# An mLSTM cell that updates its carried state every 64 tokens in place of every 128, in front of a squared-ReLU FFN

## The chip, the cores and the metric

The kernel runs on one core of one Trainium2 chip. The metric is the device time of one execution in microseconds (us); lower is better. Three timed runs of the kernel before are shown, and one further execution was taken with the hardware profiler; all durations below come from that one.

The core has five engines with a queue of their own each, and each queue is worked off in the order in which it was written: TensorE (PE, matmuls; its weight loads are shown as PEld), VectorE (DVE), ScalarE (ACT), GpSimd (POOL) and SyncE (SP, which here issues transfers). An instruction that waits holds up everything behind it in its own queue.

## The reference

There are 4 batches of 8 heads, 768 tokens and 40 dimensions per head. For every head a 40x40 state C and a normaliser n are carried over the tokens, with a running maximum m for stability, and the result goes through a two-layer FFN:

```python
for t in range(S):
    m_new = np.maximum(f_gate[:, :, t] + m, i_gate[:, :, t])
    f_stab = np.exp(f_gate[:, :, t] + m - m_new)
    i_stab = np.exp(i_gate[:, :, t] - m_new)
    m = m_new
    C = f_stab * C + i_stab * np.einsum('bhd,bhe->bhde', vt, kt)
    n = f_stab * n + i_stab * kt
    h_tilde = np.einsum('bhde,bhe->bhd', C, qt)
    nq = np.einsum('bhd,bhd->bh', n, qt)
    y[:, :, t] = sigmoid(o) * h_tilde / np.maximum(np.abs(nq), 1.0)
x = y as (4*768 tokens, 8*40)
out = np.maximum(x @ w_in, 0) ** 2 @ w_out          # w_in 320x2048, w_out 2048x320
```

Everything is float32. A recurrence of this kind can be worked off in blocks of tokens: inside a block, the output is (scores of q and k) x (a matrix W of decays, zero above the diagonal) x v; what came before the block enters as q, scaled by the decay since the block's start, times the carried C; and C is brought to the block's end once per block. n rides along as a 41st column of v that holds ones.

## The kernel before, in words

The 3072 tokens are worked off in 24 chunks of 128 (`s` is the chunk, `c = s % 6` its place in its batch), each with all 8 heads. In chunk `s` the steps are:

- `load_A`, `mask`, `decays`, `weigh`: the running log decays `A` are spread over the partitions, masked above the diagonal (POOL), exponentiated (ACT) into `eA` (the decay since the chunk's start, for q) and into W. From chunk 8 (`ROT`) on, W is laid out in 64-row halves: 192 columns a head pair, made of the two 64x64 blocks on the diagonal and the full block below it; the fourth block is zero and left out.
- `scores`: 16 matmuls of a 64x64 quarter of the array each, four of which run side by side; `weighted` (DVE) multiplies scores by W and gives P.
- `scale_q` (DVE) multiplies `eA` by q, `decay_C` (POOL) multiplies the old state by the decay over the chunk, which gives `Cd`, and `values` (POOL) scales v by the last column of W, which gives `vw`.
- `attend_begin` and `attend_end` (PE) make the output in two PSUM banks `numT`: `values_of_C` (scaled q times the old C), `values_of_P` (P times v) and `new_C` (k times `vw`). Each of the three is split over the two calls, because the two halves of a sum would otherwise be added to the same place of a bank at once. A DVE instruction on one element (the `tensor_scalar` into `spare`, line 790) stands between the two calls: it reads the last result of the first half, and the second half waits for it.
- At the end of `attend_end`, two DVE transposes (line 853) turn the output for `store_num`, and two DVE additions (line 860) write the new state, `dC + Cd`.

The order of all engines' work is written out by hand: a loop over `parts`, four steps (`at` 0 to 3) per chunk from chunk 6 on. Even chunks run beside the second FFN layer (`ffn2_fast`, line 1056), odd ones beside the first (`ffn1_open` and `ffn1_close`, line 1132, and `ffn1_rows`, line 1165), which uses Strassen-like sums made on DVE and POOL. `attend_begin` and `attend_end` stand at step 1. Between the two calls PE has other work: in an even chunk the scores of the next chunk, in an odd chunk `ffn1_rows`:

```python
if at == 1:
    do(attend_begin, s)
    if even:
        do(lambda s: scores(s, ("h", "h")), s + 1)
    if fast:
        ffn1_rows(g, 0, True)
    do(attend_end, s)
    do(decays, s + 1)
    do(mask, s + 1)
    ...
    do(decay_C, s + 1)
```

What else the change and the prediction touch:

- POOL also issues transfers: in step 3 of every even chunk `pair_up` twice (8 issues, line 343) and `load` (7 issues, lines 363 to 375), and in chunk 9, straight behind them, `spread_slots` (3 issues, lines 383 and 385; also once before chunk 6 and once in chunk 12). All of these stand in POOL's queue ahead of what the next odd chunk gives to POOL. `sums_of_x` (lines 1124 and 1127) stands just before them.
- `ffn1_open` fills four of the five PSUM banks of the pool `ps_h` (X, Y, V, Z); `ffn1_close` adds to X, Y and V, and then one ACT and four DVE instructions (lines 1182 to 1185) read them out. The next `ffn1_open` takes the fifth bank for its X and then X's, Y's and V's old banks in turn; its two DVE additions are lines 1148 and 1150.
- `keep` is a constant of ones and zeros; the scan that sums log decays restarts where it is zero, at every 128th token.

## Time and profile before

| what | value |
|---|---|
| timed runs, median (lowest to highest) | 486.21 us (484.28 to 487.42) |
| the profiled execution's own time | 486.42 us |
| its span, first to last instruction | 484.7 us |
| around the span | 1.7 us |
| granted TensorE clock | 1.00 |
| PE, DVE, ACT, POOL busy, share of the span | 98%, 71%, 50%, 46% |
| chunks 8 to 23, place in the span | about 124 to 409 us |

Busy shares are averages over the whole span. A float32 matmul shows as two records, so 16 matmuls are 32 entries in a group or a timeline. In a timeline, a row gives the start, the time from the first start to the last end, engine, line, operation, operands and the number of records; the brackets hold the idle time of the engine before it and what ended it. Because neighbouring matmuls overlap, the price of a run of them is read from its start to the start of the next run.

### The profile page before, as it was taken

To read this page: it belongs to the slowest core of one execution; us is meant where nothing else is said; L and a number is where in the kernel's file an instruction comes from. 1 tells how busy PE (TensorE), PEld (TensorE's weight loads), DVE (VectorE), ACT (ScalarE), POOL (GpSimd) and SP (SyncE) were. 2 spreads that over 40 slices of the span, in tenths; PEclk is the share of its full clock that TensorE was granted. 3 is DMA by queue.
4 is the path that set the end of the run, shared out by engine and by line. 5 is a ranking of instruction groups with operands and counts; after the bars stand their busy time and mean duration, and the time that the engine had idled before them with its cause. 6 is when DMAs were issued, how large, how long until landed. Compare 5 with 4: busy or idle time off the path is not lost.

```text
span 484.7 us, 15567 instructions
## 1 busy us (share of the span) xinstructions
PE 476.5 (98%) x6307; PEld 443.9 (92%) x6309; DVE 342.4 (71%) x722; ACT 243.2 (50%) x534; POOL 224.9 (46%) x336
## 2 busy tenths in 40 slices
PE   8999999999999999999999999999999999999997
PEld 4886787779999999999999999999999999999997
DVE  7979868798897866767775956857966956635441
ACT  4699799634743723923622931742942741513300
POOL 5464544656598096098097088089083040020000
PEclk9999999999999999999999999999999999999999
DMA  8999998788977776777677758849655612200000
GB/s 174 200 261 248 284 210 207 213 151 201 183 148 197 141 149 177 135 151 178 129 132 197 139 98 223 142 98 225 126 110 143 126 46 84 57 28 3 1 27 28
DMA packets 192696, 69.93 MB, mean 144 GB/s; under 512 B 158128, under 2 KB 181360, under 8 KB 192624
## 3 DMA queue, kind: packets, MB, share of 16 engines
q1 hardware_dynamic: 186400, 58.68, 56.0%
q0 software_dynamic: 6080, 10.16, 8.6%
q8 instruction: 50, 0.82, 0.7%
q14 instruction: 22, 0.18, 0.1%
q10 hardware_dynamic: 144, 0.10, 0.1%
HBM read 55.69 MB, written 18.92 MB: 154 GB/s over the span
## 4 chain that ended last, share of the span: by engine, by line
PE 83%; DMA 5%; DVE 4%; ACT 3%; SPq 2%; issue 1%; POOL 1%; DVEq 0%; POOLq 0%; ACTq 0%
PE h_ps L1056 32%; PE h_ps L1132 24%; PE h_ps L1165 7%; PE h_ps L972 4%; PE h_ps L1010 4%; PE numT L819 3%; PE numT L799 2%; ACT g_c L515 1%; PE numT L830 1%; DMA num_rows<-tn 1%; DMA kqT<-kq_rows 1%; PE h_ps L983 1%; PE tp L594 1%; PE h_ps L586 1%; PE tp L586 1%
## 5 line engine op out<-in xcount | busy, mean ns | idle before, releaser
L478 POOL TENSOR_SCALAR_AFFINE_SELECT A_bc<-A_bc 64x512 f32<-64x512 f32 x32 | 23.1, 721 | 88.1 <-ACT kq L496 59.3
L1146 ACT COPY r_sb<-h_ps 128x512 f32<-128x512 f32 x20 | 11.7, 585 | 84.6 <-PE h_ps L1132 84.6
L1056 PE MATMUL h_ps<-T,S 128*128 128x160 f32 x352 | 51.7, 300 | 0.0
L1056 PEld LDWEIGHTS h_ps<-T,S 128*128 128x128 f32 x352 | 48.9, 190 | 0.4 <-ACT g L1181 0.2
L1056 PE MATMUL h_ps<-w_out,g 128*128 128x160 f32 x336 | 49.2, 303 | 0.0
L1056 PEld LDWEIGHTS h_ps<-w_out,g 128*128 128x128 f32 x336 | 46.1, 190 | 1.3 <-issue 0.9
L1072 DVE TENSOR_TENSOR y_sb<-y_sb,h_ps 128x160 f32<-128x160 f32 x44 | 14.0, 318 | 45.2 <-PE h_ps L1056 45.0
L1132 PE MATMUL h_ps<-xT,w_in 128*128 128x128 f32 x320 | 43.4, 278 | 0.7 <-issue 0.7
L1132 PE MATMUL h_ps<-lent_t,w_in 128*128 128x128 f32 x320 | 42.3, 275 | 0.0
L1132 PEld LDWEIGHTS h_ps<-xT,w_in 128*128 128x128 f32 x320 | 39.2, 192 | 1.6 <-issue 1.2
L1132 PEld LDWEIGHTS h_ps<-lent_t,w_in 128*128 128x128 f32 x320 | 38.9, 192 | 0.8 <-issue 0.8
L375 POOL DMA_DIRECT2D va<-in_v_dram x64 | 39.3, 626 | 0.0
L1165 PE MATMUL h_ps<-xT,w_in 64*64 64x128 f32 x960 | 39.2, 272 | 0.0
L1132 PE MATMUL h_ps<-lent_t 128*128 128x128 f32 x320 | 39.1, 275 | 0.0
L1132 PEld LDWEIGHTS h_ps<-lent_t 128*128 128x128 f32 x320 | 37.3, 192 | 0.2 <-issue 0.2
L509 ACT ACTIVATE A_bc<-A_bc,b_R 128x64 f32<-128x64 f32 (+1 forms) x128 | 35.7, 361 | 1.0 <-POOL A_bc L478 0.6
L1165 PEld LDWEIGHTS h_ps<-xT,w_in 64*64 64x64 f32 x960 | 34.8, 133 | 1.3
L853 DVE STREAM_TRANSPOSE tn<-numT 128x256 f32<-128x256 f32 x36 | 14.0, 428 | 27.9 <-PE numT L799 18.9
L1124 POOL TENSOR_TENSOR lent_t<-xT 128x128 f32<-128x128 f32 (+1 forms) x18 | 15.6, 887 | 32.7 <-DVE xT L938 32.7
L972 PE MATMUL h_ps<-xT,w_in 128*128 128x256 f32 x128 | 30.1, 386 | 0.5 <-POOL w_in L236 0.4
L1056 PE MATMUL h_ps<-w_out,g_c 128*128 128x160 f32 x192 | 28.0, 302 | 0.0
L972 PEld LDWEIGHTS h_ps<-xT,w_in 128*128 128x128 f32 x128 | 23.4, 190 | 5.0 <-POOL w_in L236 1.3
(233 smaller groups left out, 1148.1 us busy)
## 6 DMA issues: line engine op xcount, KB each, us to landing
A_bc<-a_slots SPq DMA_DIRECT2D x32, 256.0 KB, 4.3
kq<-num_rows SPq DMA_DIRECT2D x80, 64.0 KB, 2.2
num_rows<-tn SPq DMA_DIRECT2D x18, 256.0 KB, 2.5
raw<-in_moe_w_out_dram SPq DMA_DIRECT2D x7, 640.0 KB, 5.7
kqT<-kq_rows SPq DMA_DIRECT2D x34, 128.0 KB, 3.8
og<-in_o_gate_dram SPq DMA_DIRECT2D x24, 160.0 KB, 4.9
x_rows<-x_sb SPq DMA_DIRECT2D x20, 192.0 KB, 3.4
xT<-x_rows SPq DMA_DIRECT2D x80, 48.0 KB, 3.3
```

What stands on the lines that cost most here:

```text
L375: eng.dma_start(dst[HALVES[n], PR * (1 - late_keys) : PR * (2 - late_keys)], src[HALVES[late_keys], PR * m : PR * (m + 1)],)
L478: nc.gpsimd.affine_select(part, part, compare_op=ALU.is_ge, fill=-1e30, base=0, pattern=[[0, PR], [0, 2], [1, DP]], channel_multiplier=-1,)
L509: nc.scalar.activation(A[0][:, x, to], A[0][:, x, to], AF.Exp, bias=b_R[:, b, c, own, x : x + 1],)
L819: nc.tensor.matmul(d["numT"][m][HALVES[e], i, t0:], lhsT=va_w[s % NKQ][keys, at * D1 : at * D1 + DP], rhs=rhs, start=(s % NB == 0 and i == ...
L853: nc.vector.transpose(to[:, 2 * m : 2 * m + 2], d["numT"][m].rearrange("p c t -> p (c t)"))
L972: nc.tensor.matmul(hs[i][:, n, :], lhsT=w_in[:, a, fb * P : (fb + 1) * P], rhs=xT[:, :, a, :], start=(n == 0 and a == 0), stop=False,)
L1010: nc.tensor.matmul(st["o_ps"][j], lhsT=st["g2", 0][:, fb, j * P : (j + 1) * P], rhs=w_out[:, fb, :], start=(fb == 0), stop=(fb == NF - 1),)
L1056: nc.tensor.matmul(to, lhsT=lhsT[:, p], rhs=rhs[:, p, :], start=(start and p == 0), stop=(p == NPAIR - 1), skip_group_check=True,)
L1072: add = lambda to, a, b: nc.vector.tensor_tensor(to, a, b, op=ALU.add)
L1124: sub = lambda to, a, b: eng.tensor_tensor(to, a, b, op=ALU.subtract)
L1132: nc.tensor.matmul(to[:, n, :], lhsT=lhsT[:, 4 * q + n, :], rhs=rhs, start=(start and n == 0), stop=True, skip_group_check=True,)
L1165: nc.tensor.matmul(to[cols, n, :], lhsT=w_in2[rows, 4 * q + n, cols], rhs=rhs, start=(start and n == 0), stop=True, skip_group_check=True,)
```

## The change

From chunk 8 on, the state is brought up to date after each 64 tokens. The log decays now restart at every 64th token (`keep`). Of the scores, of W and of P only the two 64x64 blocks on the diagonal are made, 128 columns a head pair in place of 192; the block below the diagonal is replaced by a second product with the state. So `attend_begin` and `attend_end` give way to `sub_begin` and `sub_end` for these chunks. `sub_begin` issues the first half's product with C, three of the four groups of P times v, and both halves of k times `vw`; then DVE adds the first half's `dC` to `Cd` and writes the state at token 64 to `mid` (which takes the place of `eA_T`, not used any more by then), and POOL multiplies `mid` by the second half's decay, which `keep_last` put aside, into a new `Cd`. `sub_end` issues the second half's products with `mid`, the rest of the first half's with C, the last of P, four transposes in place of two, and the two additions that make the new state. The one-element instruction of line 790 is gone from these chunks. The first chunk of a batch (`c == 0`) now also needs `decays`, `scale_q` and products with `mid`, and the last (`c == 5`) also `values` and the first half's k times `vw`.

```diff
--- before.py
+++ after.py
@@ -130,6 +130,12 @@
             nc.gpsimd.memset(t[:, H * D1 :], 0.0)
         nc.vector.memset(keep[:], 1.0)
         nc.vector.memset(keep[:, :, 0:1], 0.0)
+        for x in range(NX):
+            rows, whole = slice((x + 1) * BH, (x + 2) * BH), H * -(-(ROT - 2 * x) // NB)
+            nc.gpsimd.affine_select(
+                keep[rows, :, DP : DP + 1], keep[rows, :, DP : DP + 1], compare_op=ALU.is_ge, fill=0.0, base=whole - 1,
+                pattern=[[0, SX // P], [0, 1]], channel_multiplier=-1,
+            )
         make_identity(nc, ident[:])
 
         nc.gpsimd.memset(sel[:], 0.0)
@@ -482,7 +488,7 @@
 
     def decays(s):
 
-        if s % NB > 0:
+        if s % NB > 0 or s >= ROT:
             home = kq_b[2 + s % 2 if s >= NB else s - X_SQ - 1]
             e = st[s]["eA"] = home[:, 1].rearrange("p (j two) d -> p j (two d)", two=2)
             for i in range(2):
@@ -505,7 +511,7 @@
         if len(A) == 1 and not masked:
             mask(s)
         for x in range(PR if s >= ROT else 0):
-            for own, to in enumerate((slice(DP, P), slice(P, 2 * P))):
+            for own, to in enumerate((slice(DP, P), slice(P, P + DP))):
                 nc.scalar.activation(
                     A[0][:, x, to], A[0][:, x, to], AF.Exp, bias=b_R[:, b, c, own, x : x + 1],
                 )
@@ -523,10 +529,10 @@
     def values(s):
         b, c = divmod(s, NB)
         d = st[s]
-        if c + 1 < NB:
+        if c + 1 < NB or s >= ROT:
             d["vw"] = prep.tile([P, H, D1], F32, name="vw")
             if s >= ROT:
-                last = d["W"][:, :, P - 1 :: P].rearrange("p x own -> p own x")
+                last = d["W"][:, :, P - 1 : P + DP : DP].rearrange("p x own -> p own x")
                 nc.gpsimd.tensor_tensor(
                     d["vw"][:].rearrange("p (own x) d -> p own x d", own=2),
                     d["va"][:].rearrange("p (own x) d -> p own x d", own=2),
@@ -569,7 +575,7 @@
         d["sc"] = sc
         if s >= KQ_SQ:
             if s >= ROT:
-                d["sc"] = [t.rearrange("p j t -> p (j t)")[:, : 3 * P].rearrange("p (e t) -> p e t", e=2) for t in sc]
+                d["sc"] = [t.rearrange("p j t -> p (j t)")[:, : 2 * P].rearrange("p (e t) -> p e t", e=2) for t in sc]
             for e in range(2):
                 for late_keys in range(2):
                     for c in range(2):
@@ -577,14 +583,14 @@
                             rows = slice(DP * i, DP * i + D)
                             start = e == late_keys == 0
                             if s < ROT:
-                                j, keys = 2 * late_keys + e, HALVES[c]
-                                to, t0 = sc[i][HALVES[c], j, :], 0
+                                j, keys, toks = 2 * late_keys + e, HALVES[c], slice(0, P)
+                                to = sc[i][HALVES[c], j, :]
                             else:
                                 j, keys = 2 * (c ^ late_keys) + e, HALVES[late_keys]
-                                to = d["sc"][i][HALVES[c], e, slice(0, DP) if late_keys else slice(DP, 3 * DP)]
-                                t0 = DP * late_keys
+                                to = d["sc"][i][HALVES[c], e, HALVES[1 - late_keys]]
+                                toks = keys
                             nc.tensor.matmul(
-                                to, lhsT=d["kT"][rows, j, keys], rhs=d["qT"][rows, j, t0:], start=start, stop=True,
+                                to, lhsT=d["kT"][rows, j, keys], rhs=d["qT"][rows, j, toks], start=start, stop=True,
                                 skip_group_check=True,
                             )
             return
@@ -600,7 +606,7 @@
         d["P"] = []
         for i in range(2):
             heads = slice(i, H, 2)
-            t = d["W"][:, heads, :] if s < ROT else d["W"][:, i::2, DP:]
+            t = d["W"][:, heads, :] if s < ROT else d["W"][:, i::2, DP : P + DP]
             if s < W_IN:
                 at = 2 * H * P + W * (2 * (s % 2) + i)
                 t = flat_c[:, at : at + W].rearrange("p (j t) -> p j t", j=PR)
@@ -756,17 +762,114 @@
         decay_old(s + 1)
 
     def scale_q(s):
-        if s % NB > 0:
+        if s % NB > 0 or s >= ROT:
             d = st[s]
             nc.vector.tensor_tensor(d["eA"], d["eA"], d["qT"], op=ALU.mult)
 
     def decay_C(s):
+        if s >= ROT:
+            keep_last(s)
         if s % NB > 0:
-            Cd = st[s]["Cd"] = attn.tile([P, PR, D1], F32, name="Cd", bufs=1)[:]
+            d, at = st[s], (P if s < ROT else DP) - 1
+            Cd = d["Cd"] = attn.tile([P, PR, D1], F32, name="Cd", bufs=1)[:]
             nc.gpsimd.tensor_tensor(
                 Cd, C_b[(s - 1) % 2][:, : PR * D1].rearrange("p (j d) -> p j d", d=D1),
-                st[s]["eA"][:, :, P - 1 : P].to_broadcast([P, PR, D1]), op=ALU.mult,
-            )
+                d["eA"][:, :, at : at + 1].to_broadcast([P, PR, D1]), op=ALU.mult,
+            )
+
+    def keep_last(s):
+        last = st[s]["last"] = attn.tile([P, PR], F32, name="last", bufs=2)
+        nc.gpsimd.tensor_copy(last[:], st[s]["eA"][:, :, P - 1])
+
+    mid = eA_T[:].rearrange("p b c h -> p (b c h)")
+
+    def sub_matmul(s, bank, half, cols, lhsT, rhs):
+        d = st[s]
+        nc.tensor.matmul(
+            d["out"][bank][HALVES[half], cols], lhsT=lhsT, rhs=rhs, start=(bank, half) not in d["begun"], stop=True,
+            skip_group_check=True,
+        )
+        d["begun"].add((bank, half))
+
+    def sub_num(s, m, e, i, late, lhsT, rhs):
+        bank, slot = (1 - i, m) if late else (m, i)
+        at = slot * P + late * DP
+        sub_matmul(s, bank, e, slice(at, at + DP), lhsT, rhs)
+
+    def sub_C(s, late, swap):
+        C = mid if late else state(s - 1)
+        for e in range(2):
+            for i in range(2):
+                m = i ^ swap
+                j = 2 * m + e
+                sub_num(s, m, e, i, late, C[LIVE[i], j * D1 : j * D1 + DP], st[s]["eA"][LIVE[i], j, HALVES[late]])
+
+    def sub_P(s, late, swap):
+        d = st[s]
+        for e in range(2):
+            for m in range(2):
+                i = m ^ swap
+                keys, at = HALVES[m ^ late], slot(s, m, e, i, late) * D1
+                sub_num(s, m, e, i, late, va_w[s % NKQ][keys, at : at + DP], d["P"][i][keys, e, HALVES[1 - late]])
+
+    def sub_k(s, late):
+        d = st[s]
+        for e in range(2):
+            for i in range(2):
+                for m in range(2):
+                    keys, at = HALVES[m ^ late], 2 * P + (2 * late + e) * D1
+                    sub_matmul(
+                        s, m ^ late, i, slice(at, at + D1), d["kq"][keys, 0, 4 * m + 2 * e + i, :],
+                        d["vw"][keys, slot(s, m, e, i, late), :],
+                    )
+
+    def sub_begin(s):
+        c = s % NB
+        d = st[s]
+        d["out"], d["begun"] = [ps_at.tile([P, W], F32, name="numT", tag="at") for _ in range(2)], set()
+        if c > 0:
+            sub_C(s, 0, 0)
+        for late, swap in ((0, 0), (0, 1), (1, 0)):
+            sub_P(s, late, swap)
+        if c + 1 < NB:
+            sub_k(s, 1)
+        sub_k(s, 0)
+        for m in range(2):
+            dC, to = d["out"][m][:, 2 * P : 2 * P + 2 * D1], mid[:, 2 * m * D1 : 2 * (m + 1) * D1]
+            if c > 0:
+                nc.vector.tensor_tensor(to, dC, d["Cd"][:, 2 * m : 2 * m + 2].rearrange("p e d -> p (e d)"), op=ALU.add)
+            else:
+                nc.vector.tensor_copy(to, dC)
+        if c + 1 < NB:
+            Cd = d["Cd"] = attn.tile([P, PR, D1], F32, name="Cd", bufs=1)[:]
+            nc.gpsimd.tensor_tensor(
+                Cd, mid[:, : PR * D1].rearrange("p (j d) -> p j d", d=D1),
+                d["last"][:].unsqueeze(2).to_broadcast([P, PR, D1]), op=ALU.mult,
+            )
+
+    def sub_end(s):
+        c = s % NB
+        d = st[s]
+        sub_C(s, 1, 1)
+        sub_C(s, 1, 0)
+        if c > 0:
+            sub_C(s, 0, 1)
+        sub_P(s, 1, 1)
+        tn = attn.tile([P, P // SQ, PR, SQ], F32, name="tn", bufs=1)[:]
+        to = tn.rearrange("p m c r -> p c m r")
+        for bank in range(2):
+            src = d["out"][bank][:, : 2 * P].rearrange("p (c late t) -> p c late t", late=2, t=DP)
+            nc.vector.transpose(to[:, 2 * bank : 2 * bank + 2, :2], src[:, :, 0])
+            nc.vector.transpose(to[:, 1 - bank :: 2, 2:], src[:, :, 1])
+        d["tn"] = tn
+        if c + 1 < NB:
+            Cn = state(s)[:, : PR * D1].rearrange("p (m x) -> p m x", m=2)
+            for m in range(2):
+                at = 2 * P + 2 * D1
+                nc.vector.tensor_tensor(
+                    Cn[:, m], d["out"][1 - m][:, at : at + 2 * D1],
+                    d["Cd"][:, 2 * m : 2 * m + 2].rearrange("p e d -> p (e d)"), op=ALU.add,
+                )
 
     def state(s):
         return (C_b if s >= NB else C_flat)[s % 2]
@@ -1445,14 +1548,14 @@
             rounding.words()
             rounding.join()
         if at == 1:
-            do(attend_begin, s)
+            do(attend_begin if s < ROT else sub_begin, s)
             if n == 5:
                 sums_of_weights(3)
             if even:
                 do(lambda s: scores(s, ("h", "h")), s + 1)
             if fast:
                 ffn1_rows(g, 0, True)
-            do(attend_end, s)
+            do(attend_end if s < ROT else sub_end, s)
             do(decays, s + 1)
             do(mask, s + 1)
             if not even and not fast:
```

## The prediction

> **What bounds the kernel now.** I read the engines' busy shares first, then the chain of work that ended last, then the timelines of one even and one odd chunk.

> ```profile
> PE 476.5 (98%) x6307; PEld 443.9 (92%) x6309; DVE 342.4 (71%) x722; ACT 243.2 (50%) x534; POOL 224.9 (46%) x336
> PE 83%; DMA 5%; DVE 4%; ACT 3%; SPq 2%; issue 1%; POOL 1%; DVEq 0%; POOLq 0%; ACTq 0%
> ```

> PE is busy nearly always and carries 83% of the chain. So a PE microsecond saved is one off the end, if PE doesn't wait for it again, and any new PE wait is paid in full. DVE and POOL count only where they make PE wait. Chunk 10, an even one, on PE and on DVE:

> ```profile
> 167.12 0.45 PE L799 MATMUL numT<-kq,C 40*64 40x128 f32 x8
> 167.39 0.62 PE L819 MATMUL numT<-A_bc,va 64*64 64x128 f32 x16
> 167.83 0.39 PE L830 MATMUL numT<-vw,kq 64*64 64x41 f32 x16
> 168.03 0.88 PE L586 MATMUL h_ps<-kqT 40*64 40x128 f32 x32
> 168.73 0.40 PE L830 MATMUL numT<-vw,kq 64*64 64x41 f32 x16
> 168.94 0.44 PE L819 MATMUL numT<-A_bc,va 64*64 64x64 f32 x16
> 169.20 0.40 PE L799 MATMUL numT<-kq,C 40*64 40x128 f32 x8
> ...
> 168.29 0.16 DVE L790 TENSOR_SCALAR kq<-numT 1x1 f32<-1x1 f32 x1 [0.28 <-PE numT L830]
> 169.66 0.78 DVE L853 STREAM_TRANSPOSE tn<-numT 128x256 f32<-128x256 f32 x2 [1.21 <-PE numT L799]
> 170.36 0.35 DVE L860 TENSOR_TENSOR C<-numT,Cd 128x82 f32<-128x82 f32 x2
> ```

> Prices per record, from start to next start: P times v with 128 columns 0.44/16 = 27.5 ns (line 819, first row), with 64 columns 0.26/16 = 16.3 ns (line 819, second row), k times vw with 41 columns 0.20/16 = 12.7 ns. Half the columns cost 59%, not 50%.

> **PE's own work.** Records per inner chunk: scores had 16 with 128 columns and 16 with 64, and get 32 with 64; P the same; the product with C had 16 with 128 and gets 32 with 64; k keeps 32. So 32 records get cheaper by 11.2 ns (-0.36 us), and the C product goes from 16 x 27.5 to 32 x 16.3 ns (+0.08): -0.28 us for each of 11 inner chunks. The first of a batch (12, 18) gains 16 records of C (+0.26 for the 0.36 saved): -0.10. The last (11, 17, 23) gains 16 of k (+0.20): -0.08. Sum: 11 x 0.28 + 2 x 0.10 + 3 x 0.08 = **-3.5 us**.

> [...]

> **The wait in even chunks.** Today line 790 costs PE nothing in chunk 10: its 0.16 us end at 168.45, and the next chunk's scores last to 168.73. Now two additions stand there. Nearest row: line 860, the same form, 0.35 us for two, so `mid` is there at 168.64; PE restarts about 0.05 us later (chunk 14: line 790 ends at 241.88, PE starts at 241.93). The cover shrinks to 32 x 16.3 = 0.52 us, to 168.55. So PE stands for 168.69 - 168.55 = 0.14 us. Chunks 12, 14, 16, 18, 20 and 22 have the same shape: 7 x 0.14 = **+1.0**. In chunk 8, DVE is late by itself (line 790 at 131.70, after line 1072), and PE waits today; shorter multiplications in `weighted` (0.54 us for 384 columns, 0.68 for 512, so 0.40 for 256, twice 0.14 saved) about pay for the longer additions, so PE only loses its 0.25 us of gain there: **+0.25**. Bounds: 0 if the additions overlap better; 1.2 us a chunk where a 1.2 us sum (line 1051) gets ahead of them.

> **The wait in odd chunks.** `ffn1_rows` covers `mid` (1.8 us). But the new state's additions now wait for the second `Cd` from POOL, and POOL's queue is full there. Chunk 9, POOL, then DVE, then PE:

> ```profile
> 148.31 0.79 POOL L363 DMA_DIRECT2D kq<-in_k_dram  x1 [0.22 <-DMA kq_rows<-in_k_dram]
> 149.10 1.23 POOL L365 DMA_DIRECT2D kq<-in_k_dram  x2
> 150.32 2.44 POOL L375 DMA_DIRECT2D va<-in_v_dram  x4
> 152.75 0.59 POOL L383 DMA_DIRECT2D a_slots<-a_rows  x1
> 153.34 1.19 POOL L385 DMA_DIRECT2D a_slots<-a_rows  x2
> 154.54 1.41 POOL L478 TENSOR_SCALAR_AFFINE_SELECT A_bc<-A_bc 64x512 f32<-64x512 f32 x2
> ...
> 151.00 0.78 DVE L853 STREAM_TRANSPOSE tn<-numT 128x256 f32<-128x256 f32 x2 [2.29 <-PE numT L799]
> 151.71 0.35 DVE L860 TENSOR_TENSOR C<-numT,Cd 128x82 f32<-128x82 f32 x2
> 152.96 0.69 DVE L1182 TENSOR_TENSOR r_sb<-r_sb,h_ps 128x512 f32<-128x512 f32 x1 [0.90 <-PE h_ps L1132]
> ...
> 158.12 1.06 PE L1132 MATMUL h_ps<-lent_t,w_in 128*128 128x128 f32 x8
> ```

> POOL issues transfers until 154.54; only then can `Cd` start, which stands behind them and ahead of the mask. It takes 0.46 us (line 766 is 0.46 at least and 1.31 at most), plus 0.2 us for `keep_last` earlier in the queue (nearest small rows: a 32x8 select 0.18, a 128x24 memset 0.14). So DVE, standing at line 860's successor, is free for line 1182 only at 154.74 + 0.46 + 0.35 = 155.55 in place of 152.96: 2.6 us late. Behind it are lines 1183 to 1185, which free PSUM banks, and line 1148, which must read Y before PE's next product into Y (158.12 above). Line 1148 ends at 157.63 today, so 0.43 us of slack remain after 0.06 for the signal. PE comes about 0.1 us earlier. Stall: 2.6 - 0.43 + 0.1 = 2.3 us.

> The same in the other odd chunks, with the time at which POOL is free and line 1182's start: chunk 13, 226.01 and 225.66, 1.4 late, PE 0.25 earlier: 1.2 us. Chunk 19, 336.43 and 336.71, 0.7 late: 0.5. Chunk 15, 262.27 and 263.88 (0.9 of that an idle stretch put down to issue): none. Chunk 21's POOL is free in time; 11, 17 and 23 are last chunks without the second `Cd`. Sum **+4.0**. PE's idle 0.38 us in chunk 14, which DVE sets, takes up part of chunk 13's delay: **-0.4**. Bounds: 0 if DVE is late anyway; upwards, `Cd` at 1.31 and `keep_last` at 0.69 (line 147, the dearest copy).

> [...]

> **At no cost.** Transposes: 4 of half the size; from 0.43 (256 columns) and 0.56 (384) about 0.30 each, +0.35 us a chunk on DVE, in front of gaps of 0.9 (odd) and 2.3 us (before line 1072, even). ACT: 8 exponentials per chunk shrink from 386 to 337 ns; chunks 12 and 18 gain 4 at 0.41: ACT is half idle. POOL: `values` in three last chunks, 0.82 us each; the sums on lines 1124 and 1127 behind them have 2.2 us of slack there. Chunk 13's have 0.33, which would cost PE up to 0.2, contained in its 1.2. Start: three tiny selects and their wait for `keep` (DVE, until 3.06) push POOL's constants by about 1 us; they are ready at 5.4 today and needed at 7.87.

> **Sum.** -3.5 + 1.0 + 0.25 + 4.0 - 0.4 = +1.4 on the profiled 486.4, so 487.8; from the median of 486.2 it would be 487.6. I forecast **487.8**, 0.3% up, inside the 1% that a measurement of this kernel can tell from no change.

> **Rivals.** (1) DVE never stands for `Cd`, because POOL gets through its issues earlier: -3.5 + 1.0 + 0.25 = -2.2, **484.2**. For: chunks 15 and 21. Against: POOL works without a gap from 134 to 148 us. (2) The columns decide and everything is hidden: 13.9 ns for 64 columns gives 11 x 0.45 + 2 x 0.22 + 3 x 0.3 = -6.2, **480.2**. Against: 16.3 ns in every row of line 819. (3) Slower: POOL's backlog in front of the odd chunk's `Cd`. With the dear ends (`Cd` 1.31, the one in the even chunk another 0.5 of delay, `keep_last` 0.5 more) each of chunks 9, 13, 15 and 19 loses 1.85 more: 4.0 + 7.3 = 11.3, in all +8.7, **495**. It decides from 7.5 us of odd stalls on, nearly 2 us in each. (4) The blocks don't get cheaper because weight loads bind (133 ns each, four abreast 33 ns): 0 saved, then +1.4 becomes +4.9, **491.3**. Against: 16.3 is below 33.

> **Chances.** Forecast 0.46, (1) 0.19, (2) 0.09, (3) 0.22, (4) 0.04. Those within 1% (481.4 to 491.1) hold 0.66, faster 0.09, slower 0.25 (with 0.03 of (4), which lies at the edge). The range goes from 482.5, under (1), to 494, into (3).

> **What would show it.** Right: 64-column records at 16.3 ns; PE idle before the `mid` products in even chunks near 0.14; line 860's successor waiting for POOL in chunks 9, 13 and 19, with line 1182 late by 2.6, 1.4 and 0.7. Wrong: no such wait, or PE waiting in chunks 15 and 21 too, or even-chunk waits near 1 us because something stands ahead of `mid` on DVE.

## The result, and the profile after

| | kernel before | kernel after |
|---|---|---|
| median of 12 timed runs (lowest to highest) | 485.31 us (484.17 to 487.42) | 490.13 us (485.96 to 492.99) |
| ratio, 95% interval | | 1.0098 (1.007 to 1.0125) |
| the profiled execution | 486.42 us | 490.73 us |
| its span | 484.7 us | 489.0 us |

The change makes the kernel 1.0% slower. The forecast was 0.3% (487.8 us). Direction and range held, and two of the three odd-chunk stalls that were named. But of the 4.3 us by which the two profiled executions differ, 4.2 come from three places that the forecast didn't have.

The page of the kernel after, first the busy time of the engines, then the chain of work that ended last:

```profile
PE 475.0 (97%) x6613; PEld 441.8 (90%) x6613; DVE 343.6 (70%) x772; ACT 242.7 (50%) x542; POOL 238.0 (49%) x371
...
PE 77%; DVE 7%; DMA 6%; ACT 4%; POOL 2%; issue 2%; SPq 1%; DVEq 0%; POOLq 0%
```

PE works 1.5 us less than before, yet its share of the chain fell from 83% to 77%: the chain now runs over DVE, ACT and POOL more often. POOL has 13 us more to do. PE also has more instructions, 13,226 matmuls and weight loads on the page in place of 12,616, and that number matters below.

**An even chunk** goes as forecast. Chunk 10 in the timeline of PE and DVE:

```profile
168.87 0.34 PE L788 MATMUL numT<-kq,C 40*64 40x64 f32 x8
169.04 0.53 PE L788 MATMUL numT<-A_bc,va 64*64 64x64 f32 x24
...
169.39 0.63 PE L788 MATMUL numT<-vw,kq 64*64 64x41 f32 x32
169.82 0.70 PE L592 MATMUL h_ps<-kqT 40*64 40x64 f32 x32
170.06 0.39 DVE L840 TENSOR_TENSOR eA_T<-numT,Cd 128x82 f32<-128x82 f32 x2 [0.69 <-PE numT L788]
170.51 0.46 PE L788 MATMUL numT<-kq,eA_T 40*64 40x64 f32 x16
```

The 64 records of `sub_begin` last from 168.87 to 169.82, 14.9 ns each (half of them have 41 columns; the 24 of P times v take 14.6 ns each). From the start of the scores to the start of the products with `mid` (shown as eA_T) pass 0.69 us; 32 records at 16.3 ns fill 0.52. So PE stands for 0.17 us (0.11 if the records are taken at 18.0 ns, as the same 32 take in odd chunks, where nothing waits behind them). It does so in each even chunk but 8 and 18, where it is 0.3.

**Chunk 9**, an odd one, on POOL, DVE and PE:

```profile
150.05 2.60 POOL L381 DMA_DIRECT2D va<-in_v_dram  x4
...
152.64 0.59 POOL L389 DMA_DIRECT2D a_slots<-a_rows  x1
...
153.23 1.20 POOL L391 DMA_DIRECT2D a_slots<-a_rows  x2
...
154.44 0.47 POOL L845 TENSOR_TENSOR Cd<-eA_T,last 128x164 f32<-128x164 f32 x1
...
154.94 0.39 DVE L869 TENSOR_TENSOR C<-numT,Cd 128x82 f32<-128x82 f32 x2 [3.96 <-POOL Cd L845]
155.25 0.68 DVE L1285 TENSOR_TENSOR r_sb<-r_sb,h_ps 128x512 f32<-128x512 f32 x1
...
156.68 1.13 PE L1235 MATMUL h_ps<-lent_t 128*128 128x128 f32 x8 [1.98 <-DVE g L1286]
...
159.97 1.16 PE L1235 MATMUL h_ps<-lent_t,w_in 128*128 128x128 f32 x8 [0.38 <-DVE r_sb L1251]
```

Read it from the top. POOL has issued its transfers by 154.43, the second `Cd` follows, DVE has stood for it for 3.96 us, and PE, waiting for a bank that DVE's line 1286 has to read out, stands for 1.98 us. This is the wait that the prediction described. In chunk 13 it is there with 2.26 us of DVE's time and two short PE gaps; in chunk 19 DVE waits 1.08 us and PE doesn't.

**Where the time came from.** For each run of FFN matmuls, its start in the trace after minus its start in the trace before gives PE's lag, and the change of the lag from one run to the next gives what each chunk cost. For an inner chunk without any stall the lag moves by -0.14 us (even) and -0.38 (odd). What lies above that is the stall. The sections below follow chunks 9 and 13 up to a slightly later point: there the lag moved by +2.67 and +0.97, and by -0.20 without a stall (the run `loads_later`), which gives the same 2.87 and 1.17.

| where | predicted, us | measured, us |
|---|---|---|
| chunks 8 to 23 without stalls (PE's work and the even waits) | -3.5 + 1.0 + 0.25 = -2.25 | -2.94 |
| chunk 9 | +2.3 | +2.87 |
| chunk 13 | +1.2 | +1.17 |
| chunk 19 | +0.5 | 0 |
| chunk 14, an old gap that closes | -0.4 | -0.55 |
| chunk 12 | 0 | +1.52 |
| chunk 15 | 0 | +2.21, and -0.90 for a gap that was there before |
| chunk 18 | 0 | +1.40 |
| ahead of chunk 8 | 0 | -0.49 |
| sum | +1.35 | +4.29 |

The three new ones, each from the timeline. Chunk 12, POOL, ACT and PE:

```profile
193.29 1.42 POOL L484 TENSOR_SCALAR_AFFINE_SELECT A_bc<-A_bc 64x512 f32<-64x512 f32 x2
194.74 2.02 ACT L515 ACTIVATE A_bc<-A_bc,b_R 128x64 f32<-128x64 f32 x8 [1.43 <-POOL A_bc L484]
...
203.47 0.58 ACT L1284 ACTIVATE g<-h_ps 128x512 f32<-128x512 f32 x1
...
204.10 2.17 PE L1159 MATMUL h_ps<-T,S 128*128 128x160 f32 x14 [1.31 <-ACT g L1284]
```

POOL's mask comes at 193.29 (189.34 before; PE lags by only 1.7, so it is 2.3 us late). ACT has to wait for it, then works through exponentials, squares and the output gates (four tanh instructions and four scalings) without a pause until 203.47, and its relu on line 1284, which frees a PSUM bank, is late for PE. It is POOL's queue again, handed on by ACT, but without a second `Cd` in it, which chunk 11, the last of its batch, hasn't got. What the queue has got is chunk 11's `values`, new in a last chunk, which took 1.56 us (less 0.96, by which the sums behind it got shorter), and a wait for a transfer to land:

```profile
187.55 0.79 POOL L369 DMA_DIRECT2D kq<-in_k_dram  x1 [1.26 <-DMA kq_rows<-in_k_dram]
```

In the second profile of the changed kernel that wait is 0.39 us, and the stall in chunk 12 is 0.6 in place of 1.5.

Chunk 15, PE alone, and the row of the page on DMA queues that turned out to belong to it (packets, MB, share):

```profile
263.54 0.29 PE L788 MATMUL numT<-kq,C 40*64 40x64 f32 x7
265.78 0.27 PE L788 MATMUL numT<-kq,C 40*64 40x64 f32 x1 [1.96 <-issue]
```

```profile
q8 instruction: 52, 0.85, 0.7%
```

PE stops between the seventh and the eighth of eight equal matmuls, with nothing to wait for. "Issue" means that the profile has no releaser. The kernel before has a gap of 1.01 us in this chunk too, a few matmuls further on.

Chunk 18, DVE and PE:

```profile
317.66 1.25 DVE L411 STREAM_TRANSPOSE kqT<-kqT 128x1024 f32<-128x1024 f32 x1 [1.18 <-DMA kqT<-kq_rows]
...
319.27 0.89 PE L788 MATMUL numT<-A_bc,va 64*64 64x64 f32 x21 [0.86 <-DVE A_bc L614]
```

A store ahead in SP's queue took 4.0 us to land, the load of `kqT` was late, and so P was.

### The profile page after: what moved, and what is told of

It is laid out like the page before. It is cut to its first block, busy times and chain, and to the rows that moved or that the text cites. A ratio compares the mean times of both kernels' runs of the same rounds, so it can differ in the third digit from the quotient of the medians.

```text
span 489.0 us, 16260 instructions
## 1 busy us (share of the span) xinstructions
PE 475.0 (97%) x6613; PEld 441.8 (90%) x6613; DVE 343.6 (70%) x772; ACT 242.7 (50%) x542; POOL 238.0 (49%) x371
## 4 chain that ended last, share of the span: by engine, by line
PE 77%; DVE 7%; DMA 6%; ACT 4%; POOL 2%; issue 2%; SPq 1%; DVEq 0%; POOLq 0%
PE h_ps L1159 31%; PE h_ps L1235 19%; PE h_ps L1268 6%; PE numT L788 4%; PE h_ps L1075 4%; PE h_ps L1113 4%; DMA x_rows<-x_sb 2%; DMA A_bc<-a_slots 1%; PE idle L1317 1%; PE h_ps L1086 1%; PE tp L600 1%; DMA xT<-x_rows 1%; PE tp L560 1%; ACT g_c L521 1%; PE h_ps L592 1%
## 5 line engine op out<-in xcount | busy, mean ns | idle before, releaser
L845 POOL TENSOR_TENSOR Cd<-eA_T,last 128x164 f32<-128x164 f32 x13 | 6.1, 466 | 84.4 <-DVE eA_T L840 62.5
L381 POOL DMA_DIRECT2D va<-in_v_dram x64 | 39.2, 620 | 0.1
L515 ACT ACTIVATE A_bc<-A_bc,b_R 128x64 f32<-128x64 f32 x128 | 32.3, 335 | 3.8 <-POOL A_bc L484 3.5
L502 ACT ACTIVATE kq<-A_bc 64x256 f32<-64x256 f32 x64 | 23.0, 406 | 9.0 <-DMA A_bc<-a_slots 8.6
L1159 PEld LDWEIGHTS h_ps<-w_out,g_c 128*128 128x128 f32 x192 | 26.3, 190 | 0.4
```

The costliest lines, as they stand in the source:

```text
L381: eng.dma_start(dst[HALVES[n], PR * (1 - late_keys) : PR * (2 - late_keys)], src[HALVES[late_keys], PR * m : PR * (m + 1)],)
L502: nc.scalar.activation(e[rows, j : j + 2, :], A[rows, i::2, own * P : (own + 1) * P], AF.Exp)
L515: nc.scalar.activation(A[0][:, x, to], A[0][:, x, to], AF.Exp, bias=b_R[:, b, c, own, x : x + 1],)
L845: nc.gpsimd.tensor_tensor(Cd, mid[:, : PR * D1].rearrange("p (j d) -> p j d", d=D1), d["last"][:].unsqueeze(2).to_broadcast([P, PR, D1]), ...
L1159: nc.tensor.matmul(to, lhsT=lhsT[:, p], rhs=rhs[:, p, :], start=(start and p == 0), stop=(p == NPAIR - 1), skip_group_check=True,)
```

## The experiments

Three questions: is it POOL's queue (chunks 9, 13 and 12), what is the gap without a releaser, and does the change gain anything once both are out of the way? All ratios are to the kernel before, run on the same chip in the same turn. Each kernel has 12 timed runs, but `after_again` 6, `code_shifted_little` 10 and `longer_stall` 4. All kernels compute the whole reference, and added dummy matmuls feed nothing. From here on the text gives gaps of PE from the start of the last matmul to the start of the next; a row's bracket leaves out the last matmul's own time and is 0.2 to 0.3 us less.

| run | median, us | ratio (95%) |
|---|---|---|
| after_again | 488.14 | 1.0078 (1.0048 to 1.0108) |
| cd_on_vector | 484.53 | 0.9990 (0.9966 to 1.0015) |
| cd_vector_last_scalar | 484.38 | 0.9989 (0.9967 to 1.0012) |
| slots_later | 487.28 | 1.0030 (1.0006 to 1.0054) |
| longer_stall | 490.49 | 1.0123 (1.0092 to 1.0154) |
| code_shifted | 486.28 | 1.0029 (1.0010 to 1.0049) |
| before_code_shifted | 486.47 | 1.0034 (1.0014 to 1.0053) |
| code_shifted_little | 484.39 | 0.9994 (0.9974 to 1.0014) |
| loads_later | 484.44 | 0.9981 (0.9953 to 1.0008) |
| loads_later_cd_vector | 486.57 | 1.0000 (0.9970 to 1.0030) |
| before_loads_later | 483.79 | 0.9966 (0.9948 to 0.9984) |
| loads_later_shifted | 484.43 | 0.9970 (0.9947 to 0.9994) |

### The changed kernel once more

> The changed kernel once more, unaltered, for a second profile. Theory (POOL's queue): the waits of line 869 for the second Cd in chunks 9 and 13 come again, with PE standing about 2.9 and 1.2 us there, since the order in POOL's queue sets them; the ratio is again about 1.01. What is not set by the order (PE's idle 2.0 us put down to issue in chunk 15, and the late kqT load in chunk 18 with 1.5 us) is gone or in other places. Rival (all four stalls belong to the change): all come again at the same places with the same sizes.

Which of the places recur? Chunk 9's do, and cost even more: 4.23 us on the lag in place of 2.67, the fall of the clock below included. Chunk 13's do, with 0.8 us of stall, chunk 12's with 0.6 in place of 1.5, chunk 15's with a gap of 1.63. Chunk 18's doesn't (+0.07): it was one late transfer. And something new shows in the table of windows (columns: stretch, length, busy PE, PEld, DVE, ACT, POOL, then the granted TensorE clock):

```profile
155.00:160.00 5.00, 3.32 (x19) 3.35 (x20) 4.92 (x9) 3.71 (x11) 2.55 (x5) 0.75 0.52 91
160.00:165.00 5.00, 5.00 (x107) 4.88 (x110) 3.86 (x13) 2.27 (x3) 0.00 (x0) 0.91 0.47 78
```

PE's gap in chunk 9, from 153.86 to 156.68 us, was 2.82 us long here:

```profile
156.68 1.34 PE L1235 MATMUL h_ps<-lent_t 128*128 128x128 f32 x8 [2.55 <-DVE g L1286]
```

At 157.46 the granted clock fell to one half for 3.41 us, and the next two groups of eight matmuls, which take 1.06 us otherwise, took 1.91 and 1.71. So the stall is paid a second time.

### The second Cd on DVE

```diff
-            nc.gpsimd.tensor_tensor(
+            nc.vector.tensor_tensor(
                 Cd, mid[:, : PR * D1].rearrange("p (j d) -> p j d", d=D1),
```

and, in the second kernel, `keep_last` on ACT (`nc.scalar.copy`) as well.

> The second Cd is made on DVE, straight behind the two additions into mid, in place of POOL; nothing else. Theory (POOL's queue): DVE no longer stands before line 869, so PE's 2.9 us in chunk 9 and 1.2 us in chunk 13 go, for about 0.3 us of DVE time a chunk in front of gaps; 490.1 goes to about 486, a ratio to the kernel before of 1.001. Rival (the loss is the state update's own price on DVE and PE: two additions, four transposes, more and smaller matmuls): DVE gets still more work, and the ratio stays at 1.010 or rises.

> As the one with the second Cd on DVE, and keep_last moved from POOL to ACT. Theory: POOL's queue in even chunks gets shorter by the 1.05 us that keep_last takes there, so the next chunk's mask comes earlier, ACT's exponentials for chunk 12 too, and the 1.3 us for which PE waits for a bank there (ACT's relu comes late) shrink to under 0.5: about 485, ratio 0.999. Rival (chunk 12's wait is not POOL's lateness): no difference from the kernel with Cd on DVE alone.

Chunk 9 with `Cd` on DVE:

```profile
149.64 0.35 DVE L869 TENSOR_TENSOR C<-numT,Cd 128x82 f32<-128x82 f32 x2
...
150.77 0.69 DVE L1285 TENSOR_TENSOR r_sb<-r_sb,h_ps 128x512 f32<-128x512 f32 x1 [0.78 <-PE h_ps L1235]
```

Line 869 waits for nothing, and line 1285 waits for PE and not the other way round. The lag moves by +0.06 in chunk 9 and -0.20 in chunk 13, where it moved by +2.67 and +0.97. That settles the first question: one instruction of 0.47 us, behind the transfers that POOL issues up to 154.43, made both stalls. The median falls by 3.6 to 5.6 us, depending on which run of the changed kernel is taken. Moving `keep_last` as well changes nothing that can be told (0.15 us): it isn't the backlog. Chunk 12 keeps 0.5 to 0.6 us and chunk 15 its gap (1.59 and 1.28 us), so the kernel is level with the one before and not better.

### The slots' transfers behind Cd

```diff
-        if n in (12, 25):
-            spread_slots(2 + n // 25)
+        if n in (15, 31):
+            spread_slots(2 + n // 31)
```

> The changed kernel, with the three transfers of spread_slots (1.8 us on POOL) issued in step 3 of chunks 9 and 13 in place of ahead of the second Cd in chunk 9 and behind step 1 of chunk 12. Theory (POOL's queue): Cd in chunk 9 starts 1.8 us earlier, at about 152.6 in place of 154.44, and PE's stall there falls from 2.9 to about 1.0 us: ratio 1.006. Chunk 13's stall falls as well if its queue is shortened by the three issues of chunk 12 (1.2 to 0): then 1.004. Rival (DVE and PE late for other reasons): 1.010.

`Cd` of chunk 9 starts at 153.34 in place of 154.44 (PE comes to this chunk 1.1 us later here than in the first profile), DVE waits 1.77 us in place of 3.96, and the lag moves by +0.48 in place of +2.67. So every transfer ahead of `Cd` counts, not `spread_slots` alone. But the gain comes back in part in this execution: chunk 13, which was to get cheaper, costs 1.89 (0.97 before), and chunk 15's gap is 2.72.

### A longer stall in chunk 9

```diff
+            if s == ROT + 1:
+                nc.gpsimd.tensor_tensor(
+                    Cd, mid[:, : PR * D1].rearrange("p (j d) -> p j d", d=D1),
+                    d["last"][:].unsqueeze(2).to_broadcast([P, PR, D1]), op=ALU.mult,
+                )
...
```

> The changed kernel with the second Cd of chunk 9 alone written four times over on POOL instead of once, 0.47 us each, so chunk 9's V' and the close of FFN layer 1 wait 1.4 us longer; the numbers stay the same. Two things are at stake. First, that DVE's wait for POOL's Cd there is what holds PE: the PE gap of chunk 9 (2.25 to 2.82 us) grows by 1.4 to 3.7 to 4.2 us. If something else holds it the gap grows by less than 0.5. Second, the clock: in one profiled execution of the unaltered changed kernel the granted clock fell to half for 3.41 us, 0.8 us into the 2.82 us gap, and its chunk 9 cost 4.23 us instead of 2.67; 7 of 12 timed runs had a mean clock of 0.993 to 0.997, and none of 29 runs of the kernel before. If a long PE gap takes the clock down, every run here has a mean clock of 0.997 or below, and the median rises by 1.4 + 0.4 x 1.7, about 2 us, to 490 to 492.5; if the clock has another cause, the share of such runs stays near one half and the median rises by 1.4 alone, to 489.5 to 491.

The new instruction stands three times in a row, so lines behind it have numbers higher by 13 here. The row of PE behind the stall, then the windows:

```profile
157.82 2.05 PE L1248 MATMUL h_ps<-lent_t 128*128 128x128 f32 x8 [2.76 <-DVE g L1299]
```

```profile
155.00:160.00 5.00, 2.24 (x11) 2.21 (x11) 3.91 (x8) 2.56 (x10) 3.28 (x7) 0.74 0.58 102
160.00:165.00 5.00, 5.00 (x72) 4.88 (x75) 4.06 (x14) 2.81 (x3) 0.28 (x1) 0.92 0.21 19
```

DVE's wait for `Cd` is 5.29 us, 1.33 longer than in the first profile of the changed kernel, so it is POOL that holds DVE here. PE's gap is 3.04 us, only 0.8 longer and not 1.4 (0.2 longer than the 2.82 of the second profile): POOL came to `Cd` 0.47 us earlier in this execution, and a stop of 0.68 us at 152.22, put down to issue, had PE come to the gap 0.35 us later. The clock is at one half from 157.41 for 3.41 us, and all four runs have a mean clock of 0.992 to 0.997. By estimate, each fall takes 3.41 x 0.5 = 1.7 us of PE's clock, 0.35% of the span, so 0.996 is one fall and 0.993 two. Of the 12 runs of the changed kernel in the result, four had one fall by that measure and three had two; of the 29 runs of the kernel before that stood beside the first four experiments, none had any. Four runs out of four would not settle it alone, and the median, 490.49 us, lies in both of the expected ranges; the two traces say more, since the clock falls there near the gap's end or right behind it. A fall doesn't need chunk 9's gap: `cd_on_vector`, which hasn't got it, has one in 4 of its 12 runs, and `code_shifted` (below) in 8 of 12. One thing in the expectation was misread: in the first case the clock fell 0.8 us after PE had gone on, not 0.8 us into the gap.

Where a gap lies may matter too. In every trace with a clock record the clock changes only a whole number of steps of 3.413 us after it first came up (in the first profiles, before and after the change, it next changed 481.28 and 484.69 us later, 141 and 142 steps), and both falls stand 45 steps behind that. In the step that ended with the fall PE was idle for 2.55 us in `after_again` and for 2.35 us here. The 2.25 us of the first profile are cut by the border of two steps (1.69 us of idle time in the fuller one), and so are the 2.72 us in chunk 15 of `slots_later` (1.40); the fullest step without a fall has 1.83 us (`loads_later`). So the clock fell at PE gaps of 2.82 and 3.04 us and not at one of 2.72, and chunk 9's gap came with a fall in one execution of the changed kernel (2.82 us) and without one in another (2.25 us). That the gap takes the clock down is the author's reading, and two falls in traces don't prove it.

### The gap without a releaser

Three things point to PE's own program. In all five executions with the changed kernel's program (the first experiments and the result) the gap stands at the same place in PE's order, behind matmul 3,479 if the dummies at the start aren't counted, while the time at which PE goes on differs by 6.4 us. The queue "instruction" brings 52 packets of 16 KB to the changed kernel and 50 to the one before, and PE's instructions in the two traces, with its semaphore ones, are 13,412 and 12,798: one packet per 256. And the packets' own records in the trace of the changed kernel show 34 of the 45 behind 100 us beginning within 1.5 us of the moment at which PE has started 180 + 256 n instructions, but in front of the gap one began 2.44 us later, with 227 instructions started in between. So: does the gap stay in chunk 15 if PE's program is moved by some instructions?

```diff
-    idle(12)
+    idle(5)
+    short(87)
...
+    def short(n):
+        t = ps_h.tile([P, W], F32, name="idle", tag="h_ps")
+        for _ in range(n):
+            nc.tensor.matmul(
+                t[:32, :32], lhsT=zeros[:, :1].to_broadcast([P, 32]), rhs=zeros[:, :1].to_broadcast([P, 32]), start=True, stop=True,
+            )
```

(`idle(4)` and `short(112)` in the kernel before; `idle(12)` kept and `short(8)` added for the small shift. The two changed kernels have `Cd` on DVE.)

> The changed kernel with the second Cd on DVE, and with the start of TensorE's program made 160 instructions longer: of the twelve wide dummy matmuls at the start (TensorE has no data then) seven are taken out and 87 narrow ones put in, so everything behind them stands 160 instructions later in TensorE's program. Theory A (code fetch): the PE gap in chunk 15 that the profile puts down to issue (1.59 us with Cd on DVE, 2.17 in the changed kernel, 1.01 in the one before) is TensorE waiting for its own program. The instruction DMA queue brought 52 packets of 16 KB for about 13,400 TensorE instructions, one per 256; at the gap the packet came 2.4 us late and 227 instructions had been started in between. By A the gap is gone from chunk 15, since the packet border now falls elsewhere, where TensorE takes 3.8 us or more for 256 instructions, and from 484.5 us the median falls to 482 to 483.5. Theory B (something in chunk 15 itself, such as its transfers or a late result): the gap stays at 1.3 to 2 us and the time at 484 to 485.

> The kernel before, shifted by 208 TensorE instructions in the same way (eight wide dummy matmuls out, 112 narrow ones in). Theory A (code fetch): its gap of 1.01 us in chunk 15 goes, no other appears above 0.5 us, and the median falls from 485.3 to about 484 to 484.7. Theory B (the chunk itself): gap and median stay, 485 to 486. A loss at the start from the changed dummies would show ahead of 14 us and is to be read off the trace, not put to either.

> The changed kernel with the second Cd on DVE, shifted by 16 TensorE instructions alone (eight narrow dummy matmuls added). Theory A (code fetch): in chunk 15 the border still falls where 256 instructions take 2.6 us, so the gap stays at 1.2 to 2 us, and in the chunk before it at about 238 us another border now falls where 256 instructions take 2.4 us (2.9 without the shift, gap 0.3 us), so a second gap of 0.5 to 1.5 us appears there; median 484.5 to 486. Theory B (the chunk itself): one gap, in chunk 15, and nothing new at 238 us; median as without the shift, 484.5.

The gap left chunk 15 in both kernels with a large shift (no PE gap above 0.33 us in that chunk in either), and stayed, with 1.17 us, under the small one, nine matmuls nearer to the front. Nothing in that chunk was changed, so the program's place is what matters. The first transposes behind the dummies start at 5.5 to 5.9 us with and without a shift, so the dummies themselves cost nothing. In the changed kernel the hope that the gap goes for good was wrong. The row of PE in the shifted changed kernel:

```profile
334.59 0.27 PE L788 MATMUL numT<-kq,C 40*64 40x64 f32 x2 [1.85 <-issue]
```

It now stands in chunk 19, and a smaller one, of 1.07 us, at 226.0. In the kernel before, none above 0.4 us came up behind 100 us that is put down to issue; its gaps of 1.04 and 0.87 us at 103.5 and 130.6 us end with POOL's weights and with DVE's P. Yet neither median fell, as it should have by the theory: the ratios are 1.0029 against 0.9990, with intervals that just overlap, and 1.0034 for the kernel before. In the changed kernel falls of the clock (8 of 12 runs against 4) may be a part of it; in the kernel before the reason is open. The second gap that the small shift was to make at 238 us didn't come; one of 1.14 us at 153.6 did. The packets in front of these gaps, from the trace (late: from the regular point to the packet's start; started: PE instructions in that time):

| kernel | packet at, us | late, us | started | gap, us |
|---|---|---|---|---|
| before | 260.3 | 2.35 | 202 | 1.01 |
| after | 263.3 | 2.44 | 227 | 2.17 |
| cd_on_vector | 256.7 | 1.64 | 169 | 1.59 |
| slots_later | 263.0 | 3.08 | 267 | 2.72 |
| code_shifted | 223.7 | 3.12 | 246 | 1.07 |
| code_shifted | 332.0 | 2.23 | 214 | 2.07 |
| code_shifted_little | 151.2 | 2.36 | 217 | 1.14 |
| code_shifted_little | 260.3 | 1.65 | 180 | 1.17 |
| loads_later | 239.9 | 2.58 | 254 | 2.16 |
| before_loads_later, chunk 15 | 256.5 | 0.82 | 80 | none |

All traces together say it more plainly. If PE's instructions are counted from the start (matmuls, weight loads and semaphore ones), there are 26 gaps above 0.4 us between 100 and 470 us at which PE waits for no semaphore. They are spread over 12 of the 14 traces, before and after the change, with and without a shift. Every one stands behind instruction 190 to 193 of a block of 256, whatever matmul that is, and ends 2.2 to 3.9 us after a packet began (20 of them 2.2 to 2.7). This reads as PE standing at the border of a block of its program until the next one is there; no record shows the border itself.

A late packet alone is nothing rare: in the changed kernel 11 of those 45 are more than 1.5 us late, and most leave no gap. They left one where PE took its instructions fast. Behind 100 us the first profiles of the two kernels have two such gaps each (0.81 and 1.01 us before, 1.08 and 2.17 after), and there the 256 instructions from the packet's regular point on took 2.6 to 3.3 us; for every other packet over 1 us late they took 3.9 us or more. The change makes fast places: behind 100 us, the smallest time for 256 instructions is 2.11 us in its trace and 2.79 in that of the kernel before. `sub_begin` issues 64 records in 0.95 us where `attend_begin` issued 40 in 0.91.

### POOL's block of transfers moved

```diff
             do(pair_up, s + 3)
-            do(pair_up, s + 4)
-        if even and at == 3 and s > NB:
-            do(load, s + 4)
+        if not even and at == 2 and s - 1 > NB:
+            do(pair_up, s + 3)
+            do(load, s + 3)
```

> The changed kernel, second Cd on POOL as it is, with half of the block of transfers that POOL issues at the end of an even chunk s moved to the third group of the odd chunk behind it: pair_up(s + 4) and load(s + 4), which took POOL some 6.7 us (L349 x4, L369, L371 x2, L381 x4) right ahead of the odd chunk's second Cd. Theory (POOL's queue and the transfers): with the block gone from there, Cd in chunks 9 and 13 is written before DVE asks, the mask of chunk 12 is on time, and the code packet of chunk 15 no longer stands behind 1.3 MB of loads; the stalls that these made (2.9, 1.2, 1.6 and 1 to 2 us) go, the steps of -0.52 us a pair stay, and the median falls from 490 to 481 to 483.5, a ratio to before of 0.991 to 0.996. Rival 1: moving the block frees POOL but the code gap stays, since it comes from how fast the odd chunk takes its instructions: 483.5 to 485, some runs with a mean clock of 0.997 or less. Rival 2: the block lands in the way of the third group (vw, the row loads), and even chunks wait for their weights: 486 or more.

> The same move with the second Cd on DVE as well. If the move alone frees POOL's queue, this adds nothing and its median is within 0.7 us of the run with Cd on POOL. If POOL is still late for some Cd, this one is faster by the PE gap that the other shows, 1 us or more.

> The kernel before with the same move of pair_up(s + 4) and load(s + 4). It has no wait for POOL to lose, only the gap of 1.01 us in chunk 15: 484 to 485.5. If it gains as much as the changed kernel does (3 us or more), the gain is the move's and not that of the blocks; if the blocks' own steps are real, the changed kernel with the move is 2 to 4 us below this one.

Chunk 9 in the changed kernel with the move, then the one long gap that it has left:

```profile
149.50 0.36 DVE L869 TENSOR_TENSOR C<-numT,Cd 128x82 f32<-128x82 f32 x2
```

```profile
243.12 2.17 PE L1159 MATMUL h_ps<-w_out,g 128*128 128x160 f32 x14 [1.86 <-issue]
```

With `Cd` still on POOL, line 869 waits for nothing: the lag moves by -0.20 in chunks 9 and 13, and chunk 12's stall is at most 0.2. So the first theory holds from this side too. The time did not fall to the 481 to 483.5 that it asked for. A packet of program is now late in chunk 14, a place where the unmoved kernel had none; that this alone is the reason isn't shown, since the last run below takes the gap away and gains nothing. `Cd` on DVE adds nothing (with a gap of 1.37 us at the same place and one of 0.73 in chunk 15), so it is no POOL wait that is left. Its median of 486.57 is 2.1 us higher, where at most 0.7 was expected; the intervals of the two ratios overlap, and no cause was found.

The kernel before with the same move is the better one: 483.79 us, ratio 0.9966 (0.9948 to 0.9984), the narrowest spread of all kernels with 12 runs (483.39 to 485.69), and no PE gap above 0.33 us behind 100 us. Its packet in chunk 15 is 0.82 us late in place of 2.35; the move took 640 KB of loads out of that stretch. Why a packet comes late is not shown beyond that. The gain of the move isn't that of the blocks: the changed kernel with the move is 0.65 us above this one, where the blocks' own steps called for 2 to 4 us below. An estimate from the two profiled executions (483.60 and 483.39 us) says where these went: the changed one has two gaps put down to issue behind 100 us, of 2.16 and 0.54 us, and would be 2 to 2.5 us below without them.

### Move and shift together

> The changed kernel, Cd on POOL, pair_up(s + 4) and load(s + 4) moved to the third group of the odd chunk, and TensorE's program moved by 144 instructions with narrow dummy matmuls at the start (seven wide ones out, 79 narrow ones in). Without the shift its one long PE gap stood at 243 us in chunk 14 (2.16 us, put down to issue): the code packet asked for at 237.3 us began 2.58 us later with 254 instructions started in between, where 256 instructions take TensorE 2.8 us. With borders 144 instructions further on, the unshifted trace has, behind 100 us, only two stretches left in which 256 instructions take less than 4 us: at 181 us (3.3 us) and at 329 us (2.7 us). Theory (code fetch): the gap at 243 us is gone; a gap of 0.5 to 2 us appears at about 330 us in chunk 19 and perhaps one below 1 us at 184 us; median 482 to 484. If the gap at 243 us stays, the code is not its cause, and the median stays at 484 to 485.

The gap at 243 us is gone. In its place stand three of 0.6 us, at 295.7, 317.7 and 333.7 us, the last of them where one was expected (another of 0.76 at 130.2 ends with DVE's P). The kernel's ratio of 0.9970 can't be told from that of the unshifted one (0.9981): it is faster than the kernel before, by 0.3%, but not faster than the kernel before with the move (0.9966). In the changed kernel a shift spreads the late packets; it doesn't remove them. No version with 64-token updates was found that beats the kernel before with the move.

## Why the prediction was right, and where it was not

- **In short.** The mechanism held where it was named, and the time fell into the range. But +1.35 us was forecast for the profiled execution and +4.29 came; that the range, stretched to 494 for rival (3), covered it owes something to luck, since other waits than that rival's filled it.
- **PE's own work, -3.5 us, with the even waits, +1.0 and +0.25**: together -2.25 predicted and -2.94 measured. Records of 64 columns cost 14.5 to 18.0 ns in most runs of them (16.3 taken from line 819), and the wait was 0.17 us (0.14 predicted). Chunk 8's extra +0.25 didn't come (its step was -0.26), and a pair of inner chunks gained 0.52 in place of 0.42. Rival (4) is out.
- **Odd chunks, +4.0**: 2.87 + 1.17 + 0 = 4.04 measured, against 2.3 + 1.2 + 0.5. The sum is right, partly by luck, since chunk 9's excess and chunk 19's nought cancel. Chunk 9's is short by 0.6, mostly because PE came to it 0.75 us ahead of the trace before (-0.49 and -0.26 in the table), where 0.1 was reckoned with: POOL's queue sets when PE goes on, so what was gained ahead of the stall is lost in it. PE waits in two parts there, 1.98 us for line 1286 and 0.38 for line 1251, the successor of the line 1148 that the forecast went by. In chunk 19 line 1285 was only 0.3 us later than PE's own lag and the slack held. `cd_on_vector` and `loads_later` show the cause from two sides. Rival (1) described a kernel that exists: in `cd_on_vector` DVE doesn't stand for `Cd`, and its median lies 0.8 us below that of the kernel before, where the rival has 2.2.
- **`keep_last` at 0.2 us**: 0.19 in odd chunks but 1.05 to 1.14 in even ones. Without consequence there, as the run with it on ACT shows.
- **The step that failed is the forecast's limit to chunks 9, 13 and 19 for POOL's backlog, and "at no cost" for the rest.** The same queue reached the mask of the next even chunk. In chunk 12 the mask was 2.3 us late: POOL stood 1.26 us for a transfer, and `values`, priced at 0.82 us behind 2.2 us of slack, took 1.56. The mask leads to ACT, and ACT was costed as "half idle", an average over the span: there it has 8.7 us of work in one piece ahead of the relu. This cost 1.5 us, and 0.6 in the repeat.
- **A term that was missing: PE's program.** PE's instructions were priced by their time, not by their number. The gap put down to issue was seen in chunk 15 and used only as an idle stretch that relieves DVE. It grew from 1.01 to 2.17 us, and of all that the experiments took away it was the one that came back elsewhere in every profile of a changed kernel.
- **A second missing term: the clock.** The 2.3 us of chunk 9 were taken as paid once. In the second profile its gap, of 2.82 us there, came with 3.41 us at half the clock, by estimate 1.7 us more. 7 of the 12 timed runs have a mean clock of 0.997 or less, and the profiled execution hasn't; which gap it was in the timed runs isn't shown.
- **Rival (3)** had the right kind (POOL's backlog) but not the way: the second `Cd` took 0.47 us on average over its 13 times, not 1.31, and chunk 15 had no wait for it.
- Chunk 18's 1.40 us was one late transfer, and no forecast could have had it.

## What to carry to other kernels

A result that is made by a short instruction can cost what stands ahead of it in its engine's queue, transfers that this engine issues included: here 0.47 us of POOL's work on `Cd` made DVE stand for 3.96 us in chunk 9. Look for a place behind the transfers or for another engine before pricing the instruction itself. Splitting matmuls into smaller ones had a price here that their durations don't show, the number of instructions per microsecond: the program came in one packet per 256 instructions, and where packets were 1.6 to 3.1 us late PE had gaps of 1.0 to 2.7 us. All 26 stops of this kind above 0.4 us stood behind instruction 190 to 193 of a block of 256, so for a stop without a releaser it is worth counting at which instruction it stands. And when a PE stall of 2 us or more is forecast, ask what the clock will do after it: gaps of 2.82 and 3.04 us came with 3.41 us at half the clock here, gaps of 2.25 and 2.72 us did not.
